# Second layer of a two-layer block with seven products for eight, output transposed on VectorE, one join made in PSUM

## The chip, the cores and the metric

One core of a Trainium2 chip. The metric is the device time of one execution in microseconds. A ratio of two kernels is the mean time of one kernel's fast runs over the mean of the other's fast runs of the same rounds, so it is not quite the ratio of the medians that stand beside it.

## The reference, cut to what matters

```python
# 4 x 6080 tokens of 256 channels, float32
f = lb + (1 - lb) * sigmoid(f_logit);  h_t = f_t * h_{t-1} + (1 - f_t) * x_t      # recurrence
x = y.reshape(24320, 256)
h = x @ w_in            # 256 -> 2048
g = h - tanh(h)
out = g @ w_out         # 2048 -> 256
```

## The kernel before

Tokens run in blocks of 512, and d_ff in four units (u = 0 to 3) of 512. The first layer is done with seven half-size products in place of eight (sums and differences of quarter matrices are formed first and the products added up afterwards). The second layer has eight. g is computed by a polynomial: ScalarE squares h twice (t, then q), VectorE makes g out of t, q and h, half a unit at a time (the "shrink").

Names in the code: A, B and D are accumulators in PSUM, the memory into which TensorE writes its products; a bank is a piece of it of 128x512 float32, and the kernel uses eight. A11 to S4 are quarters of a weight matrix and their sums and differences, B11 to T4 those of the tokens, so A22·T4 is one of the seven products. `keep` copies a bank on ScalarE, `join` adds an earlier copy to a bank on VectorE and writes a quarter of h. fT, xT, v, scan and mix are VectorE's steps of the recurrence for the next block.

The order in which each engine gets its instructions is fixed by the program text. One pass of this loop does the first layer of unit n, the shrink of unit n-1 and the second layer of unit n-2 (guards left out, arguments shortened):

```python
for n in range(last + 1 + LAG):                 # LAG = 2
    product(n, "A", A11, "B11", start=True);  keep(n, "A", "r1")     # ScalarE copies the bank
    product(n, "D", S1, "T1", start=True);    keep(n, "D", "r5")
    join(n - 1, "A", "r5", 2)                   # VectorE: h[2] = bank A + r5
    shrink_scalar(n - 1, 0);  shrink_vector(n - 1, 0)
    second_layer(n - LAG, 0)
    product(n - 1, "A", A22, "T4")              # must wait until join A has read the bank
    nc.scalar.copy(h[3] of n - 1, bank A)
    second_layer(n - LAG, 1)
    shrink_scalar(n - 1, 1)
    product(n, "B", A12, "B21", start=True);  join(n, "B", "r1", 0)
    product(n, "A", S2, "T2");                keep(n, "A", "r2")
    shrink_vector(n - 1, 1)
    watch(n - 1, 0); watch(n - 1, 1)            # ScalarE, range check
    second_layer(n - LAG, 2)
    product(n, "D", S4, "B22");               join(n, "D", "r2", 1)
    product(n, "A", S3, "T3")
    second_layer(n - LAG, 3)
    steps(j + 1)[u]()      # next block: u=0 transpose fT and sigmoid; u=1 xT, v, scan; u=2 v, scan, mix
```

```python
# second layer: tokens on the partitions of the result
nc.tensor.matmul(ps[:, i, :], lhsT=g[:, q, c, r*P:(r+1)*P], rhs=w_out[u][:, s, c, :], ...)  # 16 a unit
```

## Time and profile before

| | us |
|---|---|
| time, median of 7 runs | 2567.6 |
| one block in the steady part | 52.24 |
| VectorE busy | 1706 (67%) |
| ScalarE busy | 1811 (71%) |

The prediction below shows the lines on which this table rests. The list of waits: the largest one and the largest one of TensorE. Left of the arrow stands who waits and for what it is about to write, right of it what ended the wait; the columns are total us, number of times and longest:

```profile
DVE q L330 <- ACT q L325: 626.4, 189, 5.4
...
PEld A L296 <- DVE h L313: 50.9, 50, 7.4
```

VectorE idles 626 us in front of the first multiplication of the shrink, because ScalarE's q is not there yet. TensorE (PEld is its weight load) hardly waits.

One line of the timeline is missing in the prediction's cut, the first matmul group of A22·T4 after the product into D at 1508.21; the 2.59 us of the prediction are its distance from there:

```profile
1510.80 1.03 PE L296 MATMUL A<-T,w_in 128*128 128x256 f32 x4
```

### The profile page before, as it was taken

The page shows a single profiled execution, that of the slowest core. Times are in us where ns is not written, and L with a number is a line of the kernel's source. Part 1 is how long each engine was busy: PE and PEld are TensorE (multiplying, and loading weights), DVE is VectorE, ACT ScalarE, POOL GpSimd, SP SyncE. Part 2 cuts the span into 40 slices and gives each one's busy share as a digit, 9 for nine tenths or more (in the row PEclk, how much of TensorE's full clock was granted, in tenths as well). Part 3 has the DMA queues.
Part 4 walks back from the last instruction along what each step waited for, and adds up shares of the span by engine and source line. Part 5 has one row for each costly group of instructions (what it writes and reads, how often), then busy time and mean ns, then how long its engine had stood idle before and what let it go on. Part 6 is the DMA issues. An engine that isn't in the chain of part 4 may idle for free.

```text
span 2565.3 us, 28917 instructions
## 1 busy us (share of the span) xinstructions
PE 2490.5 (97%) x11458; PEld 2179.2 (85%) x11458; DVE 1706.1 (67%) x1891; ACT 1810.7 (71%) x2514; POOL 0.2 (0%) x4
## 2 busy tenths in 40 slices
PE   3799999999999999999999999999999999999998
PEld 2688888888888888888888888888888888888887
DVE  7766666666666676666666666666666666667664
ACT  4677777777777777777777777777777777777775
POOL 0000000000000000000000000000000000000000
PEclk7999999999999999999999999999999999999999
DMA  6111121112111121112111211112111211112100
GB/s 156 37 25 25 25 50 25 25 26 49 26 25 25 35 39 25 25 25 50 25 25 25 43 32 25 25 26 49 25 25 25 50 26 25 25 37 38 25 9 18
DMA packets 230991, 85.05 MB, mean 33 GB/s; under 512 B 202432, under 2 KB 226752, under 8 KB 230848
## 3 DMA queue, kind: packets, MB, share of 16 engines
q1 hardware_dynamic: 230848, 83.13, 17.6%
q8 instruction: 91, 1.49, 0.3%
q14 instruction: 52, 0.43, 0.1%
HBM read 58.20 MB, written 24.90 MB: 32 GB/s over the span
## 4 chain that ended last, share of the span: by engine, by line
PE 89%; DVE 6%; ACT 3%; SPq 1%; DMA 0%; issue 0%; DVEq 0%
PE psO L361 48%; PE A L296 24%; PE D L296 11%; PE B L296 6%; DVE y L194 2%; ACT osb L373 2%; DVE h L313 1%; ACT f L177 1%; SPq L94 0%; DVE t L125 0%; DMA raw<-in_moe_w_in_dram 0%; DMA fn<-in_f_logit_dram 0%; DVE w_out L124 0%; DVE t L111 0%; DVE q L120 0%
## 5 line engine op out<-in xcount | busy, mean ns | idle before, releaser
L361 PE MATMUL psO<-w_out,h 128*128 128x256 f32 x6080 | 1442.8, 380 | 0.0
L361 PEld LDWEIGHTS psO<-w_out,h 128*128 128x128 f32 x6080 | 1160.1, 191 | 155.7
L330 DVE SCALAR_TENSOR_TENSOR q<-q,t 128x1024 f32<-128x1024 f32 (+1 forms) x384 | 464.4, 1209 | 626.4 <-ACT q L325 626.4
L296 PE MATMUL A<-T,w_in 128*128 128x256 f32 (+1 forms) x2304 | 595.2, 381 | 31.0 <-DVE h L313 30.4
L308 ACT COPY r<-A 128x512 f32<-128x512 f32 (+1 forms) x384 | 222.7, 580 | 429.9 <-PE A L296 429.9
L296 PEld LDWEIGHTS A<-T,w_in 128*128 128x128 f32 x2304 | 434.6, 192 | 107.4 <-DVE h L313 50.9
L333 DVE TENSOR_TENSOR h<-h,q 128x1024 f32<-128x1024 f32 (+1 forms) x384 | 466.2, 1214 | 13.1
L325 ACT ACTIVATE q<-t 128x1024 f32<-128x1024 f32 (+1 forms) x384 | 403.0, 1050 | 12.2
L324 ACT ACTIVATE t<-h 128x1024 f32<-128x1024 f32 (+1 forms) x384 | 403.7, 1051 | 6.6 <-DVE h L313 0.6
L339 ACT ACTIVATE junk<-t 128x1024 bf16<-128x1024 f32 (+1 forms) x384 | 403.1, 1050 | 6.0
L296 PE MATMUL A<-y,w_in 128*128 128x256 f32 (+1 forms) x768 | 197.9, 381 | 34.0 <-DVE y L194 19.4
L296 PE MATMUL D<-T,w_in 128*128 128x256 f32 (+1 forms) x768 | 197.5, 380 | 0.1
L296 PE MATMUL B<-y,w_in 128*128 128x256 f32 (+1 forms) x768 | 197.2, 380 | 0.0
L296 PE MATMUL D<-y,w_in 128*128 128x256 f32 (+1 forms) x768 | 196.0, 378 | 0.0
L296 PEld LDWEIGHTS A<-y,w_in 128*128 128x128 f32 x768 | 146.8, 193 | 54.0 <-DVE y L194 19.4
L313 DVE TENSOR_TENSOR h<-D,r 128x512 f32<-128x512 f32 (+1 forms) x192 | 131.7, 686 | 84.0 <-PE D L296 83.9
L194 DVE TENSOR_TENSOR_SCAN y<-f,y,v 128x512 f32<-128x512 f32 (+3 forms) x94 | 115.9, 1233 | 75.1 <-ACT f L177 70.0
L296 PEld LDWEIGHTS B<-y,w_in 128*128 128x128 f32 x768 | 147.2, 193 | 19.5
L296 PEld LDWEIGHTS D<-T,w_in 128*128 128x128 f32 x768 | 147.0, 193 | 19.6 <-DVE T L277 0.4
L296 PEld LDWEIGHTS D<-y,w_in 128*128 128x128 f32 x768 | 145.8, 191 | 19.3
L313 DVE TENSOR_TENSOR h<-B,r 128x512 f32<-128x512 f32 (+1 forms) x192 | 131.8, 686 | 22.5 <-PE B L296 17.8
L308 ACT COPY r<-D 128x512 f32<-128x512 f32 (+1 forms) x192 | 112.0, 583 | 40.0 <-PE D L296 39.9
(35 smaller groups left out, 818.4 us busy)
## 6 DMA issues: line engine op xcount, KB each, us to landing
fn<-in_f_logit_dram SPq DMA_DIRECT2D x188, 128.0 KB, 3.8
xn<-in_x_dram SPq DMA_DIRECT2D x188, 128.0 KB, 4.4
out_dram<-osb SPq DMA_DIRECT2D x47, 512.0 KB, 3.4
raw<-in_moe_w_in_dram SPq DMA_DIRECT2D x32, 128.0 KB, 3.5
raw<-in_moe_w_out_dram SPq DMA_DIRECT2D x8, 512.0 KB, 4.8
fn<-in_f_logit_dram SPq DMA_DIRECT2D x4, 64.0 KB, 2.6
xn<-in_x_dram SPq DMA_DIRECT2D x4, 64.0 KB, 2.2
out_dram<-osb SPq DMA_DIRECT2D x1, 256.0 KB, 2.5
```

What stands on the lines that cost most here:

```text
L177: nc.scalar.activation(out=f[:, 0:n], in_=u, func=AF.Identity, scale=nom[:, k : k + 1], bias=1.0)
L194: nc.vector.tensor_tensor_scan(out=y[:, k, a:e], data0=f[:, a:e], data1=v[:, a:e], initial=init, op0=ALU.mult, op1=ALU.add,)
L296: nc.tensor.matmul(s[bank][:, c, 0 : s["hb"]], lhsT=w_in[u][:, slot, c * P : (c + 1) * P], rhs=mixes[j][right], start=start and c == 0, st ...
L308: nc.scalar.copy(out=s[r][:, :, 0:hb], in_=s[bank][:, :, 0:hb])
L313: nc.vector.tensor_tensor(out=s["h"][:, q, :, 0:hb], in0=s[bank][:, :, 0:hb], in1=s[r][:, :, 0:hb], op=ALU.add,)
L324: nc.scalar.activation(out=t, in_=h, func=AF.Square)
L325: nc.scalar.activation(out=q, in_=t, func=AF.Square, scale=RA, bias=RB)
L330: nc.vector.scalar_tensor_tensor(out=q, in0=q, scalar=RC, in1=t, op0=ALU.add, op1=ALU.mult)
L333: nc.vector.tensor_tensor(out=h, in0=h, in1=q, op=ALU.mult)
L339: nc.scalar.activation(out=junk[:, :, :, 0:hb], in_=t, func=AF.Relu, bias=-TINY, accum_out=flags[:, 2 * n + half : 2 * n + half + 1],)
L361: nc.tensor.matmul(ps[:, i, :], lhsT=g[:, q, c, r * P : (r + 1) * P], rhs=w_out[u][:, s, c, :], start=(u == 0 and part == 0 and i % 2 == 0 ...
L373: nc.scalar.copy(out=osb[:, 0:ns, :], in_=ps[:, 0:ns, :])
```

## The change

The intent is to save two of TensorE's 16 second-layer matmuls per unit. The second layer gets seven products too, over halves of d_ff, tokens and output channels; this needs three differences of quarters of g on VectorE, sums of the seven results at the end of a block, and, since the output channels now lie on the partitions, a transpose of the output on VectorE. The four accumulators take four of the eight banks, so B and D have one bank each in place of two. The join of B moves from VectorE into PSUM: ScalarE writes the copy of A into B's bank and the product accumulates onto it.

```diff
+        def spread(n):                       # VectorE, 128x1024 + 128x512 + 128x512
...
+            for o, a, b in (
+                (T[:, 0:2], g[:, 1:3], g[:, 0:2]),
+                (g[:, 1], g[:, 2], T[:, 0]),
+                (T[:, 2], g[:, 3], g[:, 1]),
+            ):
+                nc.vector.tensor_tensor(out=o, in0=a, in1=b, op=ALU.subtract)
...
-            for b in "ABD":
-                s[b] = ps_h.tile([P, 2, HB], FP32, name=b)       # two banks each
+            s["A"] = ps_a.tile([P, 2, HB], FP32, name="A")       # two banks
+            for b in "BD":
+                s[b] = ps_b.tile([P, 2, HB], FP32, name=b)       # one bank each
...
-                    keep(n, "A", "r1")
+                    keep(n, "A", "B")
...
-                    product(n, "B", A12, "B21", start=True)
-                    join(n, "B", "r1", 0)
+                    product(n, "B", A12, "B21")
+                    keep(n, "B", 0)
...
                 if old:
                     shrink_vector(n - 1, 1)
+                    spread(n - 1)
...
+        PARTS = (                            # 14 matmuls a unit in place of 16
+            (("Qa", 0, A11, "h", 0), ("Qa", 1, S1, "T", 0)),
+            (("Qb", 0, A12, "h", 3), ("Qb", 1, S2, "h", 1)),
+            (("Qc", 0, S3, "T", 1),),
+            (("Qd", 0, S4, "h", 2), ("Qd", 1, A22, "T", 2)),
+        )
...
+            if u == NU - 1:
+                finish(j, part)   # part 0 a ScalarE copy, parts 1 to 3 VectorE sums, then the transpose
```

Cuts are marked with three dots, and the comments are mine; left out are the w_out rounding, the one-time matmul of zeros at the start, the stores, the first two differences of mix made in one instruction, and fewer buffers (t and q 2 for 3, h 3 for 5).

More of the change, by code (lines that the diff above doesn't have):

```diff
@@ L82 @@
     flag = const.tile([1, 1], FP32, name="flag")
+    zeros = const.tile([P, TB], FP32, name="zeros")
     def fetch_w_in(u, raw):
@@ L101, in fetch_w_out, with to_float32 @@
             nc.sync.dma_start(out=dst[:, s], in_=src[u, s])
-    def to_float32(dst, raw, temps):
+    def to_float32(dsts, raw, temps):
         hi = raw.bitcast(INT32).rearrange("p (n c) -> p n c", c=2)[:, :, 1]
@@ L123, in to_float32 @@
         )
-        nc.vector.tensor_tensor(out=dst, in0=r, in1=m.bitcast(INT32), op=ALU.add)
+        nc.vector.tensor_tensor(out=r, in0=r, in1=m.bitcast(INT32), op=ALU.add)
         nc.vector.scalar_tensor_tensor(
@@ L128, in to_float32 @@
         )
-        nc.vector.scalar_tensor_tensor(
-            out=dst, in0=dst, scalar=2.0**-20, in1=e, op0=ALU.mult, op1=ALU.mult
-        )
+        for dst, view in dsts:
+            nc.vector.scalar_tensor_tensor(
+                out=dst, in0=view(r), scalar=2.0**-20, in1=view(e),
+                op0=ALU.mult, op1=ALU.mult,
+            )
     def recurrence(ctx):
@@ L199, in recurrence @@
         return fetch, turn, recur, ys
-    def store(j, osb):
-        t0, nb = starts[j], sizes[j]
-        nc.sync.dma_start(
-            out=out[t0 : t0 + nb, :].rearrange("(i p) d -> p i d", p=P),
-            in_=osb[:, 0 : nb // P, :],
-        )
     @with_exitstack
@@ L219, in fast @@
         wpool = ctx.enter_context(tc.tile_pool(name="w", bufs=1))
+        rawpool = ctx.enter_context(tc.tile_pool(name="raw", bufs=3))
         mixpool = ctx.enter_context(tc.tile_pool(name="mix", bufs=2))
-        hpool = ctx.enter_context(tc.tile_pool(name="hpool", bufs=LAG + 3))
-        tpool = ctx.enter_context(tc.tile_pool(name="tpool", bufs=3))
+        hpool = ctx.enter_context(tc.tile_pool(name="hpool", bufs=LAG + 1))
+        tpool = ctx.enter_context(tc.tile_pool(name="tpool", bufs=2))
         rpool = ctx.enter_context(tc.tile_pool(name="rpool", bufs=2))
-        junkpool = ctx.enter_context(tc.tile_pool(name="junk", bufs=1))
+        sumpool = ctx.enter_context(tc.tile_pool(name="sumpool", bufs=1))
         opool = ctx.enter_context(tc.tile_pool(name="opool", bufs=2))
-        ps_h = ctx.enter_context(tc.tile_pool(name="ps_h", bufs=2, space=PSUM))
-        ps_o = ctx.enter_context(tc.tile_pool(name="ps_o", bufs=1, space=PSUM))
+        ps_a = ctx.enter_context(tc.tile_pool(name="ps_a", bufs=2, space=PSUM))
+        ps_b = ctx.enter_context(tc.tile_pool(name="ps_b", bufs=1, space=PSUM))
         w_in = [wpool.tile([P, 7, 2 * P], FP32, name=f"w_in{u}") for u in range(NU)]
-        w_out = [wpool.tile([P, 2, 2, D], FP32, name=f"w_out{u}") for u in range(NU)]
+        w_out = [wpool.tile([P, 7, 2 * P], FP32, name=f"w_out{u}") for u in range(NU)]
         A11, S3, A12, A22, S1, S2, S4 = range(7)
@@ L236, in fetch_weight @@
             kind, u = n
-            raw = hpool.tile([P, KC * TB], INT64, name="raw", tag="h")
+            raw = rawpool.tile([P, KC * TB], INT64, name="raw")
             (fetch_w_in, fetch_w_out)[kind](u, raw[:])
@@ L244, in round_weight @@
             temps = [
-                tpool.tile([P, 2, 2, HB], FP32, name=s, tag=s)[:] for s in ("t", "q", "e")
-            ]
-            if kind == 1:
-                dst = w_out[u][:].rearrange("p s c d -> p (s c d)")
-                to_float32(dst, raw[:], temps)
-                return
-            w = w_in[u]
-            dst = w[:, 0:4, :].rearrange("p n f -> p (n f)")
-            to_float32(dst, raw[:], temps)
+                pool.tile([P, 2, 2, HB], FP32, name=s, tag=s)[:]
+                for pool, s in ((tpool, "t"), (tpool, "q"), (opool, "osb"))
+            ]
+            w = (w_in, w_out)[kind][u]
+            if kind == 0:
+                dsts = [(w[:, 0:4, :].rearrange("p n f -> p (n f)"), lambda a: a)]
+            else:
+                dsts = [
+                    (
+                        w[:, 2 * s + k, :].rearrange("p (n a) -> p n a", a=H),
+                        lambda t, s=s, k=k: t[:, s * TB : (s + 1) * TB].rearrange(
+                            "p (n k a) -> p n k a", k=2, a=H
+                        )[:, :, k],
+                    )
+                    for s in range(2)
+                    for k in range(2)
+                ]
+            to_float32(dsts, raw[:], temps)
             A21 = S3
@@ L275, in mix @@
             T1, T3, T2, T4 = [T[:, n, 0:hb] for n in range(4)]
-            for o, a, b in ((T1, B12, B11), (T3, B22, B12), (T2, B22, T1), (T4, B21, T2)):
+            nc.vector.tensor_tensor(
+                out=T[:, 0:2, 0:hb], in0=y[:, :, hb : 2 * hb],
+                in1=y[:, 0, 0 : 2 * hb].rearrange("p (n t) -> p n t", n=2),
+                op=ALU.subtract,
+            )
+            for o, a, b in ((T2, B22, T1), (T4, B21, T2)):
                 nc.vector.tensor_tensor(out=o, in0=a, in1=b, op=ALU.subtract)
@@ L284, in begin @@
             s = st[n] = dict(hb=sizes[units[n][0]] // 2)
-            for b in "ABD":
-                s[b] = ps_h.tile([P, 2, HB], FP32, name=b)
-            for r in ("r1", "r2", "r5"):
+            s["A"] = ps_a.tile([P, 2, HB], FP32, name="A")
+            for b in "BD":
+                s[b] = ps_b.tile([P, 2, HB], FP32, name=b)
+            for r in ("r2", "r5"):
                 s[r] = rpool.tile([P, 2, HB], FP32, name=r)
-            s["h"] = hpool.tile([P, 4, 2, HB], FP32, name="h", tag="h")
+            s["h"] = hpool.tile([P, 4, 2, HB], FP32, name="h")
         def product(n, bank, slot, right, start=False):
@@ L303, in product, with keep @@
                 )
-        def keep(n, bank, r):
+        def keep(n, bank, to):
             s = st[n]
             hb = s["hb"]
-            nc.scalar.copy(out=s[r][:, :, 0:hb], in_=s[bank][:, :, 0:hb])
+            dst = s[to][:, :, 0:hb] if isinstance(to, str) else s["h"][:, to, :, 0:hb]
+            nc.scalar.copy(out=dst, in_=s[bank][:, :, 0:hb])
         def join(n, bank, r, q):
@@ L337, in watch @@
             hb = st[n]["hb"]
-            junk = junkpool.tile([P, 2, 2, HB], BF16, name="junk")
+            junk = sumpool.tile([P, 2, 2, HB], BF16, name="junk")
             nc.scalar.activation(
@@ L342, in watch @@
             )
+        def spread(n):
+            s = st[n]
+            hb = s["hb"]
+            s["T"] = hpool.tile([P, 3, 2, HB], FP32, name="Tg")
+            g, T = s["h"][:, :, :, 0:hb], s["T"][:, :, :, 0:hb]
+            for o, a, b in (
[9 more added lines that the diff above has]
+            (("Qd", 0, S4, "h", 2), ("Qd", 1, A22, "T", 2)),
+        )
         acc = {}
@@ L351, in second_layer @@
             j, u = units[n]
-            nb = sizes[j]
-            ns = nb // P
-            if u == 0 and part == 0:
-                acc[j] = ps_o.tile([P, NQ, D], FP32, name="psO")
-            ps, g = acc[j], st[n]["h"]
-            s, c = divmod(part, 2)
-            for i in range(ns):
-                th, r = divmod(i, ns // 2)
-                q = (0, 1, 3, 2)[2 * s + th]
-                nc.tensor.matmul(
-                    ps[:, i, :],
-                    lhsT=g[:, q, c, r * P : (r + 1) * P],
-                    rhs=w_out[u][:, s, c, :],
-                    start=(u == 0 and part == 0 and i % 2 == 0),
-                    stop=(u == NU - 1 and part == 3),
-                    skip_group_check=True,
-                )
+            s = st[n]
@@ new lines, in second_layer @@
+            hb = s["hb"]
+            products = PARTS[part]
+            if u == 0:
+                name = products[0][0]
+                acc[part] = ps_b.tile([P, 2, HB], FP32, name=name)
+            for c in range(2):
+                for _, r, slot, right, q in products:
+                    nc.tensor.matmul(
+                        acc[part][:, r, 0:hb],
+                        lhsT=w_out[u][:, slot, c * P : (c + 1) * P],
+                        rhs=s[right][:, q, c, 0:hb],
+                        start=(u == c == r == 0),
+                        stop=(u == NU - 1 and c == 1),
+                        skip_group_check=True,
+                    )
@@ L369, in second_layer, with finish, twice, add @@
+            if u == NU - 1:
+                finish(j, part)
             if part == 3:
                 del st[n]
-                if u == NU - 1:
-                    osb = opool.tile([P, NQ, D], FP32, name="osb")
-                    nc.scalar.copy(out=osb[:, 0:ns, :], in_=ps[:, 0:ns, :])
-                    store(j, osb)
+        sums = {}
+        def finish(j, part):
+            nb = sizes[j]
+            hb = nb // 2
+            Q = acc[part][:, :, 0:hb]
+            if part == 0:
+                sums["p"] = sumpool.tile([P, 2, HB], FP32, name="p15")
+                nc.scalar.copy(out=sums["p"][:, :, 0:hb], in_=Q)
+                return
+            p15 = sums["p"]
+            if part == 1:
+                sums["C"] = sumpool.tile([P, 4 * HB], FP32, name="C")
+            C = sums["C"][:, 0 : 4 * hb].rearrange("p (n t) -> p n t", n=4)
+            def twice(i):
+                return p15[:, i : i + 1, 0:hb].broadcast_to([P, 2, hb])
+            def add(o, a, b):
+                nc.vector.tensor_tensor(out=o, in0=a, in1=b, op=ALU.add)
+            if part == 1:
+                add(C[:, 0:2], Q, twice(0))
+            if part == 2:
+                add(C[:, 2], Q[:, 0], C[:, 1])
+                add(C[:, 1:4:2], C[:, 1:3], twice(1))
+            if part == 3:
+                add(C[:, 1:3], Q, C[:, 1:3])
+                osb = opool.tile([P, TB // H, KC, H], FP32, name="osb", tag="osb")
+                n = nb // H
+                nc.vector.transpose(
+                    out=osb[:, 0:n].rearrange("p j k a -> p (j k a)"),
+                    in_=sums["C"][:, 0 : 4 * hb].rearrange(
+                        "p (k j b) -> p j k b", k=KC, b=H
+                    ),
+                )
+                dst = out[starts[j] : starts[j] + nb, :].rearrange(
+                    "(j b) (i c) -> i b j c", b=H, i=G
+                )
+                for i in range(G):
+                    nc.sync.dma_start(
+                        out=dst[i],
+                        in_=osb[i * H : (i + 1) * H, 0:n].rearrange(
+                            "b j k a -> b j (k a)"
+                        ),
+                    )
@@ L400, in fast @@
             nc.vector.memset(ones[:], 1.0)
+            nc.vector.memset(zeros[:], 0.0)
+            bank = ps_b.tile([P, 2, HB], FP32, name="B")
+            nc.tensor.matmul(
+                bank[:], lhsT=zeros[:, 0:P], rhs=zeros[:], start=True, stop=True,
+                skip_group_check=True,
+            )
             fetch_weight(order[0])
@@ L435, in fast @@
                     product(n - 1, "A", A22, "T4")
-                    nc.scalar.copy(
-                        out=st[n - 1]["h"][:, 3, :, 0 : st[n - 1]["hb"]],
-                        in_=st[n - 1]["A"][:, :, 0 : st[n - 1]["hb"]],
-                    )
+                    keep(n - 1, "A", 3)
                 second_layer(n - LAG, 1)
@@ L457, in fast @@
                 if n == last + 1:
-                    most = ps_h.tile([P, 2, HB], FP32, name="most", tag="B")
+                    most = ps_b.tile([P, 2, HB], FP32, name="most", tag="D")
                     nc.tensor.matmul(
@@ L499, in general @@
                     to_float32(
-                        w[:].rearrange("p a b c -> p (a b c)"), raw[:],
+                        [(w[:].rearrange("p a b c -> p (a b c)"), lambda a: a)], raw[:],
                         [temp(s)[:] for s in ("t", "q", "th")],
@@ L557, in general @@
                 nc.scalar.copy(out=osb[:, 0:ns, :], in_=ps[:, 0:ns, :])
-                store(j, osb)
+                nc.sync.dma_start(
+                    out=out[starts[j] : starts[j] + nb, :].rearrange(
+                        "(i p) d -> p i d", p=P
+                    ),
+                    in_=osb[:, 0:ns, :],
+                )
     fast()
```

## The prediction

> **What bounds the kernel now.** I read the page's busy times first, then the chain that ended last, then the chain in order of time for the length of a block, and last the timeline of one unit. A unit is one quarter of d_ff (u = 0 to 3) for one block of 512 tokens; four units make a block, and there are 47 full blocks and a half one. From the page:
>
> ```profile
> PE 2490.5 (97%) x11458; PEld 2179.2 (85%) x11458; DVE 1706.1 (67%) x1891; ACT 1810.7 (71%) x2514; POOL 0.2 (0%) x4
> ...
> PEclk7999999999999999999999999999999999999999
> ...
> PE 89%; DVE 6%; ACT 3%; SPq 1%; DMA 0%; issue 0%; DVEq 0%
> ```
>
> TensorE is busy nearly all the time at full clock and holds 89% of the chain. So far it is plainly TensorE's kernel. The chain in order of time shows the same group of second-layer matmuls one block apart:
>
> ```profile
> 1518.73 1.74 PE psO L361 x8
> 1570.97 1.74 PE psO L361 x8
> ```
>
> A block takes 52.24 us. A unit issues 60 matmul instructions (28 in the first layer, 32 in the second; each fp32 matmul is two). The timeline repeats a unit after 12.95 us (first matmul into A at 1533.68 and again at 1546.63), so one instruction costs 12.95/60 = 0.2159 us, and four units are 51.8 of the 52.24 us. The other engines' work by shape:
>
> ```profile
> L333 DVE TENSOR_TENSOR h<-h,q 128x1024 f32<-128x1024 f32 x376 | 460.6, 1225 | 12.9
> L313 DVE TENSOR_TENSOR h<-D,r 128x512 f32<-128x512 f32 x188 | 130.0, 691 | 82.5 <-PE D L296 82.5
> L194 DVE TENSOR_TENSOR_SCAN y<-f,y,v 128x512 f32<-128x512 f32 x88 | 113.0, 1284 | 70.1 <-ACT f L177 65.3
> L180 DVE SCALAR_TENSOR_TENSOR v<-fT,om,xT 128x512 f32<-128x512 f32 x94 | 70.3, 748 | 1.7
> L158 DVE STREAM_TRANSPOSE fT<-fn 128x1024 f32<-128x1024 f32 x47 | 58.0, 1234 | 0.0
> L277 DVE TENSOR_TENSOR T<-y,T 128x256 f32<-128x256 f32 x94 | 39.7, 422 | 1.6
> ```
>
> The last columns are the mean ns of one and the idle time before. These are the prices of what the change adds. Delays between engines come from the timeline; its first column is the start in us, the second the duration:
>
> ```profile
> 1505.02 0.69 DVE L313 TENSOR_TENSOR h<-D,r 128x512 f32<-128x512 f32 x1 [0.44 <-PE D L296]
> ...
> 1505.63 1.23 DVE L158 STREAM_TRANSPOSE fT<-fn 128x1024 f32<-128x1024 f32 x1
> ...
> 1506.79 0.65 DVE L313 TENSOR_TENSOR h<-A,r 128x512 f32<-128x512 f32 x1
> 1506.90 1.06 ACT L164 ACTIVATE fT<-fT 128x1024 f32<-128x1024 f32 x1 [1.72 <-DVE fT L158]
> ...
> 1508.21 1.03 PE L296 MATMUL D<-T,w_in 128*128 128x256 f32 x4
> ...
> 1509.27 0.58 ACT L308 COPY r<-D 128x512 f32<-128x512 f32 x1 [0.28 <-PE D L296]
> 1509.75 1.06 ACT L324 ACTIVATE t<-h 128x1024 f32<-128x1024 f32 x1
> ...
> 1510.84 1.06 ACT L325 ACTIVATE q<-t 128x1024 f32<-128x1024 f32 x1
> ...
> 1511.86 0.59 ACT L436 COPY h<-A 128x512 f32<-128x512 f32 x1
> 1511.93 1.23 DVE L330 SCALAR_TENSOR_TENSOR q<-q,t 128x1024 f32<-128x1024 f32 x1 [4.49 <-ACT q L325]
> ```
>
> Read start to start: an independent VectorE instruction starts 0.08 us before its predecessor's written duration is over (0.61 after a join, 1.16 after a transpose); a dependent one starts 0.03 after it (1.26 from L330 at 1511.93 to L333 at 1513.19). ScalarE follows a matmul group by 1.06. VectorE still has long pauses (4.49 here), but only ahead of q.
>
> **What the skill says, and the trace.** The Trainium skill, "TensorE: Matmul & The Clock Gate", section "Wait — 56ns, not 53.3ns?", gives N/2.4 GHz + 2.5 ns start to start when warm. At 512 columns that is 215.8 ns; here an instruction of 256 fp32 columns takes 215.9, so it costs like 512 columns, and time follows the number of matmuls. The table at the head of that page calls ScalarE and VectorE strict FIFO; the timeline agrees, and my argument rests on it. "VectorE: DVE Perf Modes", section "Mode 2×_2P — use both read ports for one tensor", says that fp32 tensor_tensor is stuck at 1×: 1024/0.96 GHz = 1067 ns plus a fixed part, against 1225 measured, so the new differences get no faster mode. The TensorE page's Part 1 gives half clock after an idle window of about 3.4 us; the trace has no such pause in the steady part (clock 1.00), so it only bears on a rival.
>
> **The change, part by part.** *TensorE.* The second layer goes from 16 to 14 matmuls a unit: 56 instructions, 12.09 us, 48.4 us a block. Over 188 full units that removes 188 × 4 × 0.2159 = 162 us. If TensorE stayed the bound, the time would be about 2405.
>
> *VectorE.* Each unit loses the join of B (0.61 start to start; it becomes a ScalarE copy of 0.585) and gains three differences: 1.26 (128x1024), 0.72 and 0.61 (128x512). A unit becomes 0.60 (join A) + 1.26 + 1.15 + 1.26 + 1.26 (shrink) + 1.26 + 0.72 + 0.61 (differences) + 0.61 (join D) = 8.73. A block adds transposes, v, scans and mix (1.16 + 1.26 + 0.78 + 1.20 + 0.78 + 1.31 + 0.72 + 0.45 + 0.35 = 8.0) and the new finish: sums 0.61 + 0.45 + 0.61 + 0.72, output transpose 1.16 = 3.55. Total 4 × 8.73 + 8.0 + 3.55 = 46.5 us of the 48.4. By the sum VectorE just fits; but it has its waits.
>
> *Buffers, the deciding part.* Eight banks now hold A twice, B, D and four accumulators once. D is single: the next unit's first product into D waits for this unit's join of D. In VectorE's order that join comes behind the shrink of the second half and all three differences. This closes a loop from D to D that did not exist. From a unit's first matmul into D (0): ScalarE copy of D 1.06, t +0.48, q +1.09, copy of A to h +1.02, t of the second half +0.62, its q +1.09, VectorE's q +1.09: 6.45. Then q to h 1.26, h to differences 1.26, 1.26, 0.72, 0.61, join D 0.69, to TensorE 0.05: 5.85. Sum 12.30, already above 12.09. The block's other VectorE work then lies ahead of join A, on whose end TensorE's product A22·T4 and the second half's shrink hang:
> - u=0: nothing ahead but join A; 12.30.
> - u=1: the transpose fT starts at -0.13, its sigmoid at 1.14, and ScalarE does its copies of A and D only after that. Copy of A 2.17, of D 2.65, t 3.13, q 4.22, the new copy of the first sums 5.24, copy to h 5.72, t 6.34, q 7.43, VectorE 8.52 instead of 6.45: +2.07. The sums of the finish ahead of join D add 0.45 + 0.61. 15.43.
> - u=2: ahead of join A lie the last sum 0.72, output transpose 1.16, xT 1.26, v 0.78, scan 1.20. Join A starts at -0.13 + 5.12 = 4.99, ends 5.66; A22·T4 starts at 5.71 instead of 2.59: +3.12. 15.42.
> - u=3: v 0.78, scan 1.31, mix 1.52 put join A at 3.48 and A22·T4 at 4.20: +1.61. 13.91.
>
> Sum 57.06 us a block, 4.82 more than now. The steady stretch in the chain view (140.60 to 2537.19) has 46 blocks: +222. The opening gains four w_out roundings, each four strided 256-wide pieces and four differences for one 1024-wide instruction, 8 × 0.42 - 1.22 = 2.1 us, 9 in all, and the tail about 5 for the finish. 2567.3 + 222 + 9 + 5 = 2803.
>
> **The rivals.** *TensorE stays the bound*, about 2415 with opening and tail. For it: 46.5 is under 48.4, and VectorE now pauses 626 us ahead of q. Against: with in-order queues those pauses come from ScalarE's t and q, which lie in the loop above, and only about 2 us of other work per unit fits into them.
> *The plain loop holds, but the block's extra work hides in the pauses*: 4 × 12.30 = 49.2 us, about 2435. For it: after join A VectorE is free until its first q at 3.72. Against: 5.1 us in one unit and 3.6 in the next do not fit there, and join A stands behind them.
> *Throttle on top*: in u=2 TensorE pauses 5.71 - 2.59 = 3.1 us, near the skill's window. If half the clock is lost for one window per block, about 1.7 us times 47, the time is near 2880.
> *Transfers*: the output goes out in 256-byte rows in place of 1 KB rows, 73,000 more packets on 231,000. At 17.6% of the DMA engines now, I estimate 23%; hidden, no time.
>
> **Range and chances.** A loop sum of some 25 delays may be off by 0.5 us a unit, 2 us a block, 92 us in all; that gives 2710 to 2880, the top including some throttle. For the time to fall under 2516 the loop would have to be almost 6 us a block shorter than I sum it; I give this 0.08 in case I misread an order or a buffer. Within 2%: 0.06. Slower: 0.86.
>
> **What would show it.** Right: a block of about 57 us in the chain; TensorE about 2330 us busy, near 83%; VectorE near 2260 us, 81%; the leading waits of TensorE on join D (ahead of D) and on join A (ahead of A), some 8.7 us a block; the two units after the fT step and after the finish near 15.4 us, the others 12.3 and 13.9; the copy of A, t and q of ScalarE right behind the sigmoid. Wrong: a block of 48 to 50 us with TensorE over 95% busy (the loop is hidden); a clock clearly under 0.95 (throttle); D's first product starting before join D's end (the buffer is not what I think); the output transpose or the ScalarE copy into PSUM far from 1.23 and 0.59 us.

## The result, and the profile after

The changed kernel takes 2848.2 us (median of 4 runs, 2847.97 to 2849.85), against 2567.2 for the kernel before in the same rounds: ratio 1.110, 95% interval 1.108 to 1.112. It is slower by 11%. The prediction was 2803, range 2710 to 2880.

First the page of the changed kernel: busy times, granted clock, and the chain that ended last.

```profile
PE 2484.6 (87%) x10756; PEld 2078.2 (73%) x10756; DVE 2238.6 (79%) x2496; ACT 1871.7 (66%) x2706; POOL 0.2 (0%) x4
...
DVE 44%; ACT 27%; PE 20%; issue 7%; DMA 1%; SPq 1%; DVEq 0%
```

TensorE lost instructions (10,756 for 11,458) and is no longer the chain: its share fell from 89% to 20%, and VectorE and ScalarE hold 71% between them although neither is busy more than 79% of the time. ("issue" is time in which an engine waited for nothing that the profile shows.) A chain that hops between two engines which both have time to spare is a chain of latencies. The list of waits says where TensorE stands:

```profile
DVE q L347 <- ACT q L342: 520.1, 257, 3.7
...
PEld A L311 <- DVE h L330: 217.1, 86, 9.1
...
PE A L311 <- DVE h L330: 179.1, 81, 8.9
PEld D L311 <- DVE h L330: 173.3, 158, 3.0
...
PE D L311 <- DVE h L330: 103.8, 47, 2.6
```

L330 is the line of both joins. TensorE waits on the join of D ahead of its first product into D, and on the join of A ahead of A22·T4. VectorE's own wait for q fell by only 106 us: its added work did not go into that pause.

One transition, from u=1 to u=2, in the timeline of the changed kernel (start, duration, engine, and in brackets the idle time before):

```profile
1512.45 1.03 PE L311 MATMUL A<-y,w_in 128*128 128x256 f32 x4
...
1514.94 0.68 DVE L330 TENSOR_TENSOR h<-D,r 128x512 f32<-128x512 f32 x1
1515.55 0.68 DVE L434 TENSOR_TENSOR C<-Qd,C 128x512 f32<-128x512 f32 x1
...
1515.68 1.13 PE L311 MATMUL D<-T,w_in 128*128 128x256 f32 x4 [2.21 <-DVE h L330]
1516.26 1.25 DVE L445 STREAM_TRANSPOSE osb<-C 128x1024 f32<-128x1024 f32 x1
...
1517.43 1.20 DVE L161 STREAM_TRANSPOSE xT<-xn 128x1024 f32<-128x1024 f32 x1
...
1518.67 0.75 DVE L183 SCALAR_TENSOR_TENSOR v<-fT,om,xT 128x512 f32<-128x512 f32 x1
...
1519.52 1.28 DVE L197 TENSOR_TENSOR_SCAN y<-f,y,v 128x512 f32<-128x512 f32 x1
...
1520.72 0.67 DVE L330 TENSOR_TENSOR h<-A,r 128x512 f32<-128x512 f32 x1
...
1521.44 1.13 PE L311 MATMUL A<-T,w_in 128*128 128x256 f32 x4 [1.50 <-DVE h L330]
```

Read it as a queue: after the join of D (1514.94) VectorE does the last sum, the output transpose, xT, v and the scan, and only then the short join of A (1520.72), for which TensorE has been standing still for 1.50 us. A22·T4 starts 5.76 us after the product into D (1515.68 to 1521.44), where it was 2.59 before and 5.71 in the prediction. Everything that hangs on A22·T4 (a copy, a square, q, the second half of the shrink, the differences, the next join of D) moves back with it.

The times from one unit's first product into D to the next's can be read off this timeline, and stand against the prediction's sums:

| from unit | predicted | measured (start to start) |
|---|---|---|
| u=0 | 12.30 | 1545.37 to 1557.78: 12.41 |
| u=1 | 15.43 | 1500.38 to 1515.68: 15.30 |
| u=2 | 15.42 | 1515.68 to 1531.26: 15.58 |
| u=3 | 13.91 | 1531.26 to 1545.37: 14.11 |
| block | 57.06 | 57.40 |

This block took 57.40 us. By the starts of the output transpose, two blocks in three take 58.36 us instead, and the mean from 239.27 to 2734.32, 43 blocks, is 58.02. The other 0.6 us has another cause, which the view by stretches shows. Its columns after the window are its length, the busy us of TensorE, its weight loads, VectorE, ScalarE and GpSimd, then the granted clock, and the DMA figures:

```profile
1513.30:1515.68 2.38, 0.17 (x1) 0.00 (x0) 2.35 (x5) 0.57 (x1) 0.00 (x0) 1.00 0.00 0
1515.68:1516.65 0.97, 0.97 (x4) 0.87 (x5) 0.94 (x2) 0.00 (x0) 0.00 (x0) 1.00 0.00 0
1516.65:1520.06 3.41, 3.29 (x9) 2.10 (x7) 3.27 (x4) 2.60 (x3) 0.00 (x0) 0.55 0.33 71
```

After TensorE's pause the clock drops to about half for 3.4 us (the trace's clock record has 0.50 from 1516.98 to 1520.40). In this block the slow matmuls end in the next pause and cost nothing; where the slow stretch lies on A22·T4 and what follows, the block is 0.96 us longer. The clock record bears this out in all 43 blocks: in the 16 of 57.4 to 57.5 us the slow stretch ends at most 4.3 us after the output transpose begins, and in the 27 longer ones it begins at 4.3 us or later and lasts to 8 or more; A22·T4 starts 5.2 us after the output transpose here. The mean clock of the run is 0.952, against 0.989 before.

### The profile page after: what moved, and what is told of

Read it like the earlier page. It is cut to its first block, busy times and chain, and to the rows that moved or that the text cites. A ratio compares the mean times of both kernels' runs of the same rounds, so it can differ in the third digit from the quotient of the medians.

```text
span 2846.2 us, 28332 instructions
## 1 busy us (share of the span) xinstructions
PE 2484.6 (87%) x10756; PEld 2078.2 (73%) x10756; DVE 2238.6 (79%) x2496; ACT 1871.7 (66%) x2706; POOL 0.2 (0%) x4
## 2 busy tenths in 40 slices
DMA packets 306257, 85.03 MB, mean 30 GB/s; under 512 B 302016, under 2 KB 302016, under 8 KB 306112
## 3 DMA queue, kind: packets, MB, share of 16 engines
q1 hardware_dynamic: 306112, 83.14, 15.6%
## 4 chain that ended last, share of the span: by engine, by line
DVE 44%; ACT 27%; PE 20%; issue 7%; DMA 1%; SPq 1%; DVEq 0%
ACT t L341 10%; DVE Tg L373 9%; ACT q L342 8%; DVE q L347 8%; DVE h L350 8%; PE A L311 7%; DVE h L330 6%; PE D L311 5%; DVE h L373 4%; PE Qa L399 4%; DVE y L197 4%; ACT h L325 3%; DVE fT L161 2%; PE Qb L399 2%; ACT r L325 2%
## 5 line engine op out<-in xcount | busy, mean ns | idle before, releaser
L311 PE MATMUL A<-T,w_in 128*128 128x256 f32 (+1 forms) x2304 | 630.9, 398 | 202.1 <-DVE h L330 179.1
L311 PEld LDWEIGHTS A<-T,w_in 128*128 128x128 f32 x2304 | 441.9, 199 | 315.0 <-DVE h L330 217.1
L342 ACT ACTIVATE q<-t 128x1024 f32<-128x1024 f32 (+1 forms) x384 | 402.7, 1049 | 12.2
L399 PE MATMUL Qb<-h,w_out 128*128 128x256 f32 (+1 forms) x1536 | 394.4, 404 | 0.0
L373 DVE TENSOR_TENSOR Tg<-h 128x512 f32<-128x512 f32 (+2 forms) x384 | 365.0, 950 | 13.1
L399 PEld LDWEIGHTS Qb<-h,w_out 128*128 128x128 f32 x1536 | 316.4, 208 | 49.9
L311 PEld LDWEIGHTS D<-T,w_in 128*128 128x128 f32 x768 | 134.2, 193 | 185.4 <-DVE h L330 173.3
L325 ACT COPY h<-A 128x512 f32<-128x512 f32 (+1 forms) x192 | 111.7, 582 | 238.2 <-PE A L311 238.2
L325 ACT COPY B<-A 128x512 f32<-128x512 f32 (+1 forms) x192 | 109.0, 568 | 241.8 <-PE A L311 241.7
L399 PE MATMUL Qa<-Tg,w_out 128*128 128x256 f32 (+1 forms) x768 | 243.6, 401 | 0.0
L399 PE MATMUL Qa<-h,w_out 128*128 128x256 f32 (+1 forms) x768 | 239.8, 395 | 0.0
L399 PE MATMUL Qd<-h,w_out 128*128 128x256 f32 (+1 forms) x768 | 227.8, 378 | 0.0
L399 PE MATMUL Qd<-Tg,w_out 128*128 128x256 f32 (+1 forms) x768 | 227.7, 378 | 0.0
```

What stands on the lines that cost most here:

```text
L311: nc.tensor.matmul(s[bank][:, c, 0 : s["hb"]], lhsT=w_in[u][:, slot, c * P : (c + 1) * P], rhs=mixes[j][right], start=start and c == 0, st ...
L325: nc.scalar.copy(out=dst, in_=s[bank][:, :, 0:hb])
L342: nc.scalar.activation(out=q, in_=t, func=AF.Square, scale=RA, bias=RB)
L373: nc.vector.tensor_tensor(out=o, in0=a, in1=b, op=ALU.subtract)
L399: nc.tensor.matmul(acc[part][:, r, 0:hb], lhsT=w_out[u][:, slot, c * P : (c + 1) * P], rhs=s[right][:, q, c, 0:hb], start=(u == c == r == ...
```

## The experiments

Each was run beside the kernel before, on one chip with the others of its group, and timed in three rounds. The kernel before had medians of 2567.6 to 2569.9 us in these groups. In the expectations, k1, k5 and k6 are experiments 1, 5 and 6.

### 1. Join of A ahead of the block's other work

```diff
                     product(n, "A", S3, "T3")
+                    join(n, "A", "r5", 2)          # was: join(n - 1, ...) after the other work
                 second_layer(n - LAG, 3)
```

> The changed kernel with one instruction moved: the join of A on VectorE goes right behind the join of D, ahead of the block's other work; no work is added or removed. My theory (the order on VectorE and ScalarE sets the end): the wait of TensorE on the join of A goes; the units u=0 to 3 take 12.4, 15.9 (the sigmoid now comes 0.6 later), 13.9 and 12.5 us, 54.8 a block for 58.0 measured in the changed kernel, so about 2700 us (2680 to 2730). Rival 'VectorE's sum of work is the bound': the sum is unchanged, so 2848. Rival 'the stores in 256-byte rows or the ScalarE copy into PSUM cost the time': 2848.

Measured: 2687.1 us (ratio to before 1.046), correct. The blocks take 54.83 and then 54.60 us, the predicted 54.8. One instruction of 0.67 us per unit moved, no work removed: 161 us gained. So neither the sum of VectorE's work nor the stores nor the copy into PSUM can be what set the end; the order on VectorE did, at least for this part. The half-clock stretches nearly went too (mean clock 0.982), which is part of the gain.

### 2. Without the three differences (wrong results on purpose)

```diff
-                    spread(n - 1)
...
-            (("Qa", 0, A11, "h", 0), ("Qa", 1, S1, "T", 0)),
+            (("Qa", 0, A11, "h", 0), ("Qa", 1, S1, "h", 1)),     # and so for Qc and Qd
```

> Wrong results on purpose: the three differences on VectorE (1.26 + 0.72 + 0.61 us a unit) are left out and the products read h in their place; the matmuls, the finish and all else stay. My theory: they lie in the loop from join D to join D, but without them TensorE takes over in three units, and in u=2 it still waits for the join of A; about 50.3 us a block, 2490 us (2440 to 2600), with a wait of 2 us or more on the join of A left in one unit per block. Rival 'VectorE's sum is the bound': 58.0 - 10.4 = 47.6, so TensorE's floor of 48.4 us a block, 2405. Rival 'the finish, the stores or the PSUM join cost the time': near 2848.

Measured: 2531.5 us (0.986), a block of 51.11 us, for 50.3 expected; inside the range. Leaving out 10.4 us of VectorE work per block gains 6.9 us, and TensorE is still not at its floor of 48.4: it keeps the wait on the join of A, once in a block, 143.8 us in 50 times by its list of waits. With VectorE busy only 70% the loss of 2.7 us per block cannot be called one of throughput.

### 3. Two banks for D (wrong results on purpose)

```diff
-            (("Qc", 0, S3, "T", 1),),
+            (("Qa", 1, S3, "T", 1),),               # frees Qc's bank
...
+            for b in "AD":
+                s[b] = ps_a.tile([P, 2, HB], FP32, name=b)      # D doubled
```

> Wrong results on purpose: the Qc product is accumulated into Qa's bank, and the bank so freed is given to D, which then has two. My prediction called the single D bank the deciding part; if so, most of the 5.8 us a block goes: 2600 or less. Reckoned again from the trace: the first square of a unit needs the join of D too, so the same loop closes over ScalarE without D's bank; only u=0 gains 0.4 us, 56.95 for 57.4 us, and perhaps some of the half-clock windows: 2795 to 2830.

Measured: 2847.2 us (1.109), for 2848.2 with one bank: no gain. The time is 17 us above the range I had given, so even the small gain did not come. The timeline of this kernel, at the same transition, says why:

```profile
1513.42 1.03 PE L311 MATMUL D<-T,w_in 128*128 128x256 f32 x4
...
1521.56 2.07 PE L311 MATMUL A<-T,w_in 128*128 128x256 f32 x4 [5.09 <-DVE h L330]
```

The first product into D no longer waits, and the whole pause reappears ahead of A22·T4, 5.09 us in one piece; the changed kernel's next block, whose pauses no slow stretch shortens, has 2.21 ahead of D and 2.90 ahead of A22·T4, 5.11 together. The longer pause is followed by more half clock (mean 0.934; the four matmul instructions take 2.07 us for 1.13), and nearly all blocks take 58.03 us, where the changed kernel has a third at 57.4. So the few tenths that I expected in u=0 may be there, hidden by the clock; the 5.8 us a block that the bank would have given back, had it been the cause, are not. This kernel's list of waits has what took the bank's place, a wait of ScalarE's first square for the same join, which the changed kernel has once, for 2.4 us:

```profile
ACT t L341 <- DVE h L330: 35.2, 47, 2.4
```

The bank was not the cause that my prediction made of it.

### 4. Filler matmuls in the pause

```diff
+                if new and u == 2 and j > 0:
+                    for _ in range(6):
+                        nc.tensor.matmul(acc[2][:, 1, 0:HB], ..., start=False, stop=True)
                 if old:
                     product(n - 1, "A", A22, "T4")
```

> Six matmuls into the unused half of Qc's bank are put ahead of TensorE's product A22*T4 in u=2, 2.6 us inside a wait of 2.9 us. If the half-clock windows that each block shows cost time, they go or get fewer, all blocks take 57.4 us or a little less in place of 57.4 and 58.36, and the time falls by about 30 us to 2818 (2805 to 2830), clock above 0.97. Rival 'the half clock lies beside the path': 2848 or, with the added work, more.

Measured: 2852.4 us (1.111). A miss. The clock rose to 0.972, but the time did not fall:

```profile
1517.39 1.96 PE L311 MATMUL D<-T,w_in 128*128 128x256 f32 x4 [2.21 <-DVE h L330]
1519.14 1.06 PE L399 MATMUL Qa<-h,w_out 128*128 128x256 f32 x2
...
1521.77 2.75 PE L530 MATMUL Qc<-y,w_in 128*128 128x256 f32 x12
1524.36 1.03 PE L311 MATMUL A<-T,w_in 128*128 128x256 f32 x4
```

The pause ahead of D alone is enough for a slow stretch in this block, and then the filler ends at about 1524.4, after the moment at which A22·T4 would have run. These blocks take 58.5 us; the others take 57.41, as in the changed kernel. A filler of this length is no way to save the loss; and as it delays A22·T4 itself, this run doesn't measure what the slow stretches cost. That is read from the two block lengths of the changed kernel alone.

### 5. Experiment 1 with the sigmoid later

```diff
-            if s == 0:
-                u = dst[:, 0:n]
-                nc.scalar.activation(out=u, in_=u, func=AF.Sigmoid, scale=-1.0)   # ahead of the next copies
...
                     keep(n, "A", "r2")
+                    if u == 1 and j + 1 < NBLK:
+                        sigmoid(j + 1)
```

> k1 with ScalarE's sigmoid for the next block issued one unit later, ahead of the watches, in place of ahead of the copies of A and D. Nothing is added or removed. My theory: u=1 falls from 15.9 to 13.8 us, the others stay; 52.4 us a block for 54.6 in k1: 2585 us (2565 to 2610). Rival 'the sum of VectorE's or ScalarE's work is the bound': 2687 as in k1.

Measured: 2593.2 us (1.010), a block of 52.65 us. Nothing but the place of 47 ScalarE instructions changed, and 94 us went, for 102 expected. ScalarE is busy 72% of the span here; it was the queue position that cost.

### 6. Joins of D and A ahead of the differences and of two sums

```diff
                     shrink_vector(n - 1, 1)
-                    spread(n - 1)
...
                     product(n, "D", S4, "B22");  join(n, "D", "r2", 1)
                     product(n, "A", S3, "T3");   join(n, "A", "r5", 2)
+                if old:
+                    spread(n - 1)
+                # sums 2 and 3 of the finish here too
```

> k5 with the joins of D and A ahead of the three differences, and the second and third sums of the finish behind them. The differences leave the loop from unit to unit (TensorE needs them 0.9 us later than the join of D and in pieces), so plain units become TensorE's 12.09 us; in u=2 and u=3 VectorE is still about 1 us late with the differences. About 50.5 us a block: 2490 us (2460 to 2530), under the 2567 of the kernel before. Rival 'the differences on VectorE cost what they cost wherever they stand': 2585.

Measured: 2462.8 us (0.959), a block of 49.98 us; range 2460 to 2530. With the differences and the second and third sums of the finish behind the joins (the run doesn't tell their shares apart), the chain that ended last is TensorE's again, and the kernel is faster than the one before:

```profile
PE 88%; DVE 9%; issue 1%; ACT 1%; SPq 1%; DMA 0%; DVEq 0%; ACTq 0%
```

### 7. The block's other work dealt evenly over the four units

```diff
-            return {0: first, 1: second, 2: third}       # fT | xT, v, scan | v, scan, mix
+            # u=3: output transpose, fT of two blocks on;  u=0: xT, v, scan;
+            # u=1: sums of the finish;                     u=2: v, scan, mix
```

> k6 with the block's other work dealt evenly: output transpose and the fT of two blocks on in u=3, xT with v and the first scan in u=0, sums of the finish in u=1, v with the second scan and mix in u=2. Work unchanged, at most 3.8 us beside the 8.7 in any unit. My theory: every unit fits TensorE's 12.09 us, 48.4 to 49 us a block: 2400 us (2385 to 2440), TensorE over 95% busy and no half-clock windows in the middle. Rival 'at 46.5 of 48.4 us VectorE cannot run without 5% of waits': 2470 or more.

Measured: 2389.5 us (0.930, interval 0.929 to 0.932), correct. A block takes 48.35 us, TensorE's floor of 48.4. The view by stretches of this kernel:

```profile
1500.00:2000.00 500.00, 500.00 (x2319) 440.14 (x2318) 472.72 (x521) 401.10 (x581) 0.00 (x0) 1.00 0.16 33
```

TensorE is busy 500.00 of 500 us at full clock, with VectorE at 472.7, 95%. This is the whole gain that the change aimed at, with the change's own instructions. Here VectorE at 95% and ScalarE at 80% do not hold TensorE up, because what TensorE waits for stands early enough in their queues.

### 8. The kernel before with the three differences added

```diff
                     shrink_vector(n - 1, 1)
+                    dead_differences(n - 1)      # same three shapes, into a tile that nobody reads
                     watch(n - 1, 0)
```

> The kernel before with the three differences added on VectorE behind the shrink of the second half, written to a scratch tile that nobody reads; TensorE keeps its 60 instructions, its banks and its output path. My theory (the differences ahead of the join of D lengthen the chain join D, square, shrink, join D): although VectorE's sum is only 45 of 52 us, u=1 to u=3 take 13.7 to 14.1 us, about 54.5 a block: 2670 us (2600 to 2720). Rival 'the loss comes from the finish, the single D and B banks or the join in PSUM': 2567 to 2580.

Measured: 2763.8 us (1.075), correct. The direction and the mechanism are as expected and the size is not: it lies above my range. The blocks take 55.44 and 57.13 us in turn. Two of its waits:

```profile
PEld A L297 <- DVE h L314: 206.3, 96, 7.4
...
DVE h L314 <- PE B L297: 176.9, 96, 3.8
```

The first is the known one. The second I had left out of the sum: in the kernel before, the join of B stands on VectorE ahead of the second half's shrink and waits there for TensorE's product into B, which now comes late because A22·T4 does. The clock has a part as well: by the trace's clock record each of the 22 blocks of 57.1 us holds one stretch of 3.4 us at half clock and no block of 55.44 holds any, so about 1.69 us in every second block, 37 us in all, is the clock's; the rest of the excess over 54.5 us a block is in all blocks. With VectorE at 79% and ScalarE at 65%, and with its old banks and output path, this kernel lost 7.5% to three instructions per unit in the wrong place and to the slow stretches after its pauses.

### 9. The changed kernel with the join of B back on VectorE

```diff
-                    keep(n, "A", "B")
+                    keep(n, "A", "r1")
...
-                    product(n, "B", A12, "B21");             keep(n, "B", 0)
+                    product(n, "B", A12, "B21", start=True); join(n, "B", "r1", 0)
```

> The changed kernel with one part undone: the join of B is made on VectorE again, as in the kernel before, in place of ScalarE's copies into and out of B's bank. My theory: the join stands in VectorE's order ahead of the second half's shrink and waits there for TensorE's product into B, so each unit's loop grows by 0.3 to 0.5 us, 1.5 us a block, and the half-clock windows around that product now fall on the path, up to 1 us more: 2930 us (2900 to 2970). Rival 'ScalarE's write into PSUM and the accumulation onto it cost time, or it makes no difference': 2850 or less.

Measured: 2930.1 us (1.141), blocks of 58.99 and 60.47 us. So the join in PSUM helps as it stands: it is worth about 80 us here. What it takes out of VectorE's queue is a wait for the product into B, 169.5 us in 96 times in this run's list and gone from the changed kernel's. The clock is not the reason: the blocks without slow matmuls on A22·T4 are 58.99 us here and 57.4 there.

| kernel | us | a block |
|---|---|---|
| before | 2567.6 | 52.24 |
| changed | 2848.2 | 57.4 and 58.36 |
| 1: join of A first | 2687.1 | 54.6 |
| 5: and sigmoid later | 2593.2 | 52.65 |
| 6: and both joins ahead of the differences | 2462.8 | 49.98 |
| 7: and other work dealt evenly | 2389.5 | 48.35 |

## Why the prediction was right, and where it was not

**What bounds the kernel before.** Right: TensorE, and its 14 matmuls per unit do cost 48.35 us a block once nothing holds them up (experiment 7).

**The loop.** Right in its sum. 57.06 us was predicted for a block and 57.40 measured where no slow stretch intervened. TensorE's weight loads waited 390 us for the two joins (217.1 and 173.3), 8.3 a block for the 8.7 forecast. The small excess of 0.34 fits, without being shown by a run, what each restart costs: ScalarE's copy starts 1.17 us after the first matmul when TensorE has just waited (1521.44 to 1522.61), for the 1.06 that I had read in a stretch without waits. The parts proved themselves one by one: the order ahead of the join of A (experiment 1), the sigmoid ahead of the copies (experiment 5), the differences ahead of the join of D (experiments 2 and 8, and 6 together with two sums).

**"Buffers, the deciding part. D is single."** Wrong. Experiment 3 gave D its second bank, and the time stayed: 2847.2 us for 2848.2, where the bank as the cause meant 2600 or less. The same chain closes without the bank: the first square of a unit reads h[1], which the join of D writes, so ScalarE waits for that join in any case, and A22·T4 waits for the join of A behind it. The step that failed is the one that called a wait the cause because it was the first in a row; removing it moved the pause, 5.09 us in one piece, to the next wait of the same chain. The order on VectorE and ScalarE was what cost: the three moves of experiments 1, 5 and 6 took 161, 94 and 130 us away with D still single.

**The throttle.** Put down as a rival worth 80 us and left out of the central figure. It is there: half clock for 3.4 us after the pauses, and 0.62 us a block on average (58.02 less 57.40), 29 us over 46 blocks. With 0.34 for the restarts, 16 us, this is the 45 us between 2803 and 2848. The term was left at zero; it measured 29. The sign that I had set for it, a clock clearly under 0.95, did not come (0.952) though the loss did.

**VectorE's prices.** Right: the differences took 1225 and 692 ns, the output transpose 1245, ScalarE's copy into PSUM 572. VectorE was busy 2239 us for the 2260 estimated. TensorE's busy time was estimated at 2330 and is 2485, because the profile counts slow and restarted matmuls longer (the same 10,756 instructions are busy for 2316 us in experiment 7); it is no measure of work here. The 1067 ns in the prediction is an estimate from the page's clock alone; the measured 1225, the same for the old multiplication and the new difference, is what counts.

**The rivals.** "TensorE stays the bound" and "the extra work hides in the pauses" are refuted for the order as written, and experiments 6 and 7 show that they come true for another order. The second of these rested on the 626 us of VectorE's pause; that pause could be filled after all, down to 71 us in experiment 7, but only by work that stands behind the joins in the queue. "Transfers": hidden, as predicted; the estimate of 23% was wrong, the DMA share is 15.6%. The packets rose from 230,991 to 306,257, but the DMA engines' time did not: 17.6% of 2565 us before and 15.6% of 2846 us after, 451 and 444 us.

**Two slips of arithmetic.** 2803 and 92 are 2895, so the top of the range, 2880, is not the sum's error with throttle added. And 2516 lies 6.2 us a block below 2803, not "almost 6".

What stays open: the pauses after which the clock drops were not varied one by one, so no rule for them follows from these runs. A pause of 2.21 us ahead of D was followed by half clock in the block shown; in the next block the same pause was not, and the clock dropped only within the 2.90 us ahead of A22·T4.

## What to carry to other kernels

When work is added to an engine that has idle time, ask where in its queue the instruction stands on which the bound engine waits; put the short producer (here two joins of 0.67 us) ahead of the long work that nobody needs yet, and deal the long work evenly. A wait that heads a chain of waits need not be its cause: take it away in an experiment before paying for it with a buffer. And check a change that loses for an order in which it wins: here the same instructions ran from 11% slower to 7% faster.

## What the Trainium skill lacked or had wrong

- "TensorE: Matmul & The Clock Gate", Part 1, has the clock fall to half after at least one idle window of about 3.4 us, and the page's closing table warns of gaps over about 3 us. Here it fell after shorter pauses: TensorE paused 2.2 us, ran 0.97 us of matmuls, and then got 0.55 of the clock for 3.41 us. The window before the drop was not idle: it holds 1.1 us of matmuls (0.17 and 0.97 in 3.35 us). A later passage of the same part, on PSUM-queue cycling, does tell of a clock that swings when TensorE idles only briefly between groups, but gives no length for the pauses. That the slow stretch lasts about 3.4 us agrees with the page.
